# Bank order, copy order and late rounding around the gated block of a fused attention + SwiGLU kernel

## The chip, the cores and the metric

The kernel runs on one core of one Trainium2 chip. The metric is the device time of one launch in microseconds (us), as the median of several runs. The engines are named as in the profile: PE (TensorE: matmuls; PEld is its weight loads), ACT (ScalarE), DVE (VectorE), POOL (GpSimd) and SP (SyncE, which here only issues DMAs).

## The reference

```python
# attention: B, H, S, D = 4, 8, 768, 64; a query sees the keys that fall in its own hash bucket
mask = q_bucket[:, :, :, None] == k_bucket[:, :, None, :]
scores = np.where(mask, scale * (q @ k.T), -1e9)
x = softmax(scores) @ v                 # -> (3072 tokens, 512)
# gated block: w_gate, w_val (512, 1536), w_out (1536, 512), all float64 inputs
g = x @ w_gate
y = (g * (1.0 / (1.0 + np.exp(-g))) * (x @ w_val)) @ w_out     # -> (3072, 512), float32
```

## The kernel before

**Three stages.** Attention comes first (to about 314 us of the profiled span). Then the 3072 tokens go through the gated block in three blocks of 1024: block 0 (314 to 513 us), block 1 (513 to 715 us), and a last block that uses a seven-product scheme with sums of weights and of inputs (715 us to the end). The change touches the gated block alone.

**Split numbers.** A matmul operand is held in three parts along an index v: 0 high, 1 low, 2 their difference ("diff"). A product needs four matmul passes on the parts 0 and 1 ("a") and one set on part 2 ("n"), and the two results are joined as (4096+1)·a − n.

**Order.** The order is written out by hand: every engine runs its instructions in the order in which the Python emits them. A waiting instruction therefore holds back all that is queued behind it on its engine.

**U steps.** A U step (function `up` and the U branch of `atoms_of`) makes 128 columns of gate and value for 1024 tokens. It has four atoms, at = 0 to 3, in the order of PE: a of the gate, a of the value, n of the gate, n of the value. After each a, ACT copies it times −4097 into the bank pair of the same side's n (L847), so that the n matmuls add onto it. After n of the gate, ACT takes its Silu (L860); after n of the value, DVE multiplies it by the gate (L870). Later ACT makes the high part of the hidden value (L879), and DVE the low part and the diff (L890, L893); this "tail" is emitted two atoms after the step.

**D steps.** After every third U step, one U later, a D step multiplies three hidden tiles by three pieces of w_out. It goes through eight chunks c of 128 tokens, nine matmuls each: six into half 0 of a bank pair (a), three into half 1 (n). ACT (L956), or DVE for some parts (L958), evicts half 0 into the running sum, then DVE subtracts half 1 (L962). In block 1, D steps after the first add onto a sum: `sow` has ACT copy −sum into half 1 of the chunk's bank pair before its matmuls (L921), called from `ahead_of["D"]` inside the U step before, from `begin` and from `chunk`. D 3, the last of a block, starts with two of the three j of the first chunks (`begin`), since its third hidden tile is not ready. In what follows, "D 0 of block 1" is the first D step of block 1, and so on.

**Banks.** PSUM is used as four bank pairs, given in turn by `two_banks` (a counter modulo four). A U step takes four, a D step eight, so U always begins at the same pair, called bank 0 here, and chunk c of a D step stands in bank c mod 4. Before, a U step held a of the gate in bank 0, n of the gate in bank 1, a of the value in bank 2, n of the value in bank 3.

**Ring.** Weights come in pieces of 768 KB through a ring of six buffers. `bring` (L308) asks for the next piece on POOL's queue; the request waits until the buffer's last reader is done.

**Sums.** During block 1, DVE also makes the sums of weights (tile `made`, side g and side v, `add`, L1079 to L1088) and of inputs (xa, xb, ya, yb; L1096 to L1102) that the last block needs. ACT rounds their high part (`high`, L1108), DVE the rest (`low`, L1114 or L1116; `diff`, L1123 or L1127), and SP stores them (L1125, 1536 KB; L1129, 768 KB each). There is one `made` buffer for a side, so the next sum of that side waits until the store before has landed. The dictionary `plan`, filled by `put(kind, f, at, op, ...)`, says after which atom each of these is emitted.

**Last block.** `group("g" or "v", p)` runs the seven products A11, S1, S2, A12, S3, S4, A22 with the operands T1 to T4 (loaded by L1177 and L1205) and emits left-over work of the group before at slots 1 to 6 (`then`, `at_slot`).

```python
ahead_of["D"] += [lambda: sow(1), lambda: sow(2 if order[i + 1][1] % 4 < 3 else 3)]   # L1215
tails.append([1 if n % NF == NF - 1 else 2, tail])                                    # L1248
```

Of the kernel before, what the change touches and what calls it, by code (L numbers as in the profile page):

```python
# [19 lines left out]
def kernel(  # L20
# [33 lines left out]
    B, H, S, D = q.shape  # L54
# [12 lines left out]
    NQ = 3  # L67
# [724 lines left out]
    def gated_block(scope):  # L792
# [12 lines left out]
        def mm(ps, w, x, start, stop, **more):  # L805
            nc.tensor.matmul(ps, w, x, start=start, stop=stop, **more)  # L806

        def up(F, what):
            b = F // NF
            w = held[what, F]  # L810
            a, n_ = two_banks("a"), two_banks("n")

            def block(v, j):
                return w[:, v, j * P : (j + 1) * P]

            def first():
                for j in range(NJ):
                    for v in range(2):
                        for half in range(WB // PIECE):
                            mm(a[:, half], block(v, j), r32(xparts[b, j][:, half, v]),  # L820
                               j == 0 and v == 0, j == NJ - 1 and v == 1)

            def second(onto):
                for j in range(NJ):
                    for half in range(WB // PIECE):
                        mm(n_[:, half], block(2, j), r32(xparts[b, j][:, half, 2]),
                           j == 0 and not onto, j == NJ - 1, skip_group_check=onto)

            return first, second, a, n_
# [4 lines left out]
        def atoms_of(kind, n):  # L834
# [66 lines left out]
            else:  # L901
# [24 lines left out]
                def start(c, js, steps=None):  # L926
                    if c not in tiles:
                        tiles[c] = two_banks("o")
                    t = tiles[c]
                    cols = slice(c * P, (c + 1) * P)  # L930
                    def first():
                        for j in js:
                            for v in range(2):
                                mm(t[:, 0], hs[j][:, v, cols], ws[j][:, v],
                                   j == 0 and v == 0, j == nq - 1 and v == 1)

                    def second():
                        for j in js:
                            mm(t[:, 1], hs[j][:, 2, cols], ws[j][:, 2], j == 0 and not onto,
                               j == nq - 1, skip_group_check=onto)  # L940

                    for go in steps or ("ba" if final and c >= ahead else "ab"):
                        (first if go == "a" else second)()

                def end(c):
                    t = tiles.pop(c)
                    early = final and c >= ahead
                    if early:
                        nc.vector.tensor_tensor(accs[c], accs[c], t[:, 1], op=ALU.subtract)
                    if part == 0 or onto:  # L950
                        if part == 0 and c // 2 not in paired:
                            accs[c // 2, "both"] = outp.tile([P, 2, DM], FP32, tag=f"o{c // 2}",
                                                             name="o")
                        if part == 0:
                            accs[c] = accs[c // 2, "both"][:, c % 2]
                        nc.scalar.activation(accs[c], t[:, 0], AF.Copy, scale=STEP + 1)  # L956
                    else:
                        nc.vector.scalar_tensor_tensor(out=accs[c], in0=t[:, 0],  # L958
                                                       scalar=STEP + 1, in1=accs[c],
                                                       op0=ALU.mult, op1=ALU.add)  # L960
                    if not early:
                        nc.vector.tensor_tensor(accs[c], accs[c], t[:, 1], op=ALU.subtract)  # L962
                    if part == NF // nq - 1:
                        batch, at = divmod(b * NCB + c, NCH)
                        if final and c >= ahead:
                            nc.sync.dma_start(rows[batch][:, at, :], accs[c])
                        elif c // 2 in paired:
                            nc.sync.dma_start(rows[batch][:, at - at % 2 : at - at % 2 + 2, :], accs[c // 2, "both"])
                    paired.add(c // 2)
                    if c == NCB - 1:  # L970
                        bring(nq)

                def begin(c):
                    sow(ahead)
                    start(c, range(nq - few))
                    if c == ahead - 1:
                        sow(4)

                for c in range(ahead):
# [27 lines left out]
                for c in turns_:  # L1007
                    if final and c == NCB - 1:
                        yield lambda: last(NCB - 1)
                        return  # L1010
                    if final and c == NCB - 2:
                        last_diffs(NCB - 1)

                    def chunk(c=c):
                        if c >= ahead:
                            start(c, range(nq))
                        else:
                            start(c, range(nq - few, nq), "ab")
                        if ahead and c == 5:
                            sow(7)  # L1020
                        end(c)
                        if not ahead:
                            sow(c + 3)
                        elif c >= ahead:
                            sow(8 if c >= 5 else c + 2)
                    yield chunk

        bring(RINGS[1])
# [116 lines left out]
        for p in range(NG - 1):  # L1145
            g, v = ("w", p, 0), ("w", p, 1)
            F = (LAST - 1) * NF + 2 * p
            put("U", 2 * p, 0, keep_w, "g", F)
            put("U", 2 * p, 1, keep_w, "v", F)
            f = 2 * p + 1  # L1150
            if f % NQ == 0:
                at = [("D", f // NQ - 1, c) for c in range(1, 6)]
            else:
                at = [("U", f + 1, c) for c in range(1, 4)]
                at += [("D", f // NQ, 0), ("D", f // NQ, 1)] if (f + 1) % NQ == 0 else [("U", f + 2, 0), ("U", f + 2, 0)]
            ops = [[(high, g)], [(high, v), (low, g)], [(diff, g)], [(low, v)], [(diff, v)]]
            for here, todo in zip(at, ops):
                for op, key in todo:
                    put(*here, op, key)
# [1 line left out]
        put("U", 4, 2, load_x, LAST, (1, 1 + NP // 2))  # L1161
        xa, xb, ya, yb = (("x", j, side) for j in range(2) for side in range(2))
        for kind, f, at, op, key in (("U", 4, 0, add, xa), ("U", 4, 1, add, xb),
                                     ("U", 4, 2, high, xa), ("U", 4, 3, high, xb),
                                     ("U", 4, 3, low, xa), ("U", 4, 3, diff, xa),
                                     ("U", 5, 0, low, xb), ("U", 5, 0, diff, xb),
                                     ("D", 1, 3, add, ya), ("D", 1, 5, add, yb),
                                     ("D", 1, 5, high, ya), ("D", 1, 7, high, yb),
                                     ("D", 1, 6, low, ya), ("D", 1, 7, diff, ya),
                                     ("U", 7, 0, low, yb), ("U", 7, 0, diff, yb)):  # L1170
            put(kind, f, at, op, key)
# [39 lines left out]
        def sow_next(i):  # L1211
            if i + 1 < len(order) and order[i + 1][0] == "D":
                gens[i + 1] = atoms_of(*order[i + 1])
                sow = next(gens[i + 1])
                ahead_of["D"] += [lambda: sow(1), lambda: sow(2 if order[i + 1][1] % 4 < 3 else 3)]  # L1215

        for i, (kind, n) in enumerate(order):
            b, f = divmod(n, NF if kind == "U" else NF // NQ)
# [19 lines left out]
            for at, atom in enumerate(gens.pop(i, None) or atoms_of(kind, n)):  # L1238
# [12 lines left out]
                if kind == "D" and f == NF // NQ - 1:  # L1251
                    if at == 0:
                        more = [split_x(b + 1, pr) for pr in range(NP // 2, NP)]
                        if b == LAST - 1:
                            for i_ in (1, 2):
                                bring_sum(i_, xparts_p, f"x{i_ - 1}")
                    if b == LAST - 1:
                        if at in (2, 4, 5, 7, 8, 9):
                            more[at in (4, 7, 9)].pop(0)()
                        if at == 7:  # L1260
                            fourth_sum()
                    elif at in (0, 7, 10):
                        for x in more:
                            x.pop(0)()
# [40 lines left out]
        def then(k, op):  # L1305
            after.setdefault(k, []).append(op)
# [5 lines left out]
        def group(what, p):  # L1312
# [125 lines left out]
            then(3, lambda: diff(0))  # L1438
            then(3, lambda: high(1))
            then(4, lambda: low(1))  # L1440
            then(5, lambda: diff(1))

        gates = {}
        assert not tails
# [47 lines left out]
```

## Time and profile before

| what | value |
|---|---|
| median of 3 runs | 905.1 us (904.12 to 906.36) |
| the profiled execution's own time | 903.35 us |
| its span, first to last instruction | 901.3 us |
| PE busy | 891.0 us, 99% |
| DVE busy | 678.9 us, 75% |
| ACT busy | 533.5 us, 59% |
| POOL busy | 106.7 us, 12% |
| granted TensorE clock | 0.999 |
| DMA, all queues | 224.06 MB, mean 249 GB/s |

The span and what lies around it differ by 2.05 us in the profiled execution. A busy engine is one that works on an instruction; a PE matmul of 512 columns counts as about 390 ns although the next one starts 227 ns later (32 matmuls of a U step at 346.68 to 353.93 us), since they overlap in the pipeline. So lost time on PE shows as a start that comes later than 227 ns after the last one, more fully than as idle time.

### The profile page before, as it was taken

Reading aid. Unit: us, or ns where it says so; the run is one execution under the profiler, and the core shown is the slowest. Engines: PE = TensorE matmul, PEld = TensorE weight load, DVE = VectorE, ACT = ScalarE, POOL = GpSimd, SP = SyncE. Lnnn points to the kernel's source line nnn. Section 1 sums busy time; section 2 is a strip of 40 time slices with the busy share of each in tenths; the row PEclk is TensorE's granted clock in tenths of the full one; section 3 lists DMA queues with packets and bytes.
Section 4 is the critical chain, followed back from the end, with each engine's and each line's share of the span. In section 5 each row is a group of like instructions: output and inputs, shape, how many; then the busy total and the mean of one; then the engine's idle time right before and its main releaser. Section 6 shows DMA issues by size and latency. Waiting matters only on the chain.

```text
span 901.3 us, 12795 instructions
## 1 busy us (share of the span) xinstructions
PE 891.0 (99%) x4731; PEld 622.4 (69%) x4731; DVE 678.9 (75%) x877; ACT 533.5 (59%) x782; POOL 106.7 (12%) x211
## 2 busy tenths in 40 slices
PE   9999999999999999999999999999999999999998
PEld 5444444444444487888878788878888777888887
DVE  6779999999988956649473987789793578377486
ACT  7788988788888745442433234446364576376470
POOL 2001100010001210001001000100010122121110
PEclk9999999999999999999999999999999999999999
DMA  7657877887877699685857788797869998297382
GB/s 183 109 148 183 188 205 190 214 217 215 231 193 219 210 361 349 235 301 174 295 194 257 251 342 323 255 348 304 325 266 400 393 357 280 86 350 263 138 300 93
DMA packets 149980, 224.06 MB, mean 249 GB/s; under 512 B 104000, under 2 KB 113696, under 8 KB 148000
## 3 DMA queue, kind: packets, MB, share of 16 engines
q0 software_dynamic: 25312, 128.99, 40.7%
q1 hardware_dynamic: 123200, 93.08, 34.0%
q10 hardware_dynamic: 1408, 1.20, 0.5%
q8 instruction: 37, 0.61, 0.3%
q14 instruction: 23, 0.19, 0.1%
HBM read 157.81 MB, written 64.59 MB: 247 GB/s over the span
## 4 chain that ended last, share of the span: by engine, by line
PE 72%; DVE 12%; issue 8%; DMA 4%; ACT 2%; POOL 1%; SPq 0%; POOLq 0%; DVEq 0%; ACTq 0%
PE sc L605 17%; PE av L636 14%; PE o L806 13%; PE a L806 13%; PE n L806 6%; PE y L806 3%; DMA sums_ram<-made 2%; PE joint L677 1%; DVE hid L1410 1%; PE joint L497 1%; DMA ring<-sums_ram 1%; DVE o L962 1%; DVE made L1114 1%; DVE made L1123 1%; DVE hid L890 1%
## 5 line engine op out<-in xcount | busy, mean ns | idle before, releaser
L806 PE MATMUL o<-ring,hid 128*128 128x512 f32 (+1 forms) x872 | 201.3, 389 | 4.2 <-ACT g L860 2.2
L806 PEld LDWEIGHTS o<-ring,hid 128*128 128x128 f32 x872 | 162.0, 188 | 42.2 <-ACT o L921 3.9
L806 PE MATMUL a<-xparts,ring 128*128 128x512 f32 x768 | 178.1, 389 | 0.0
L806 PEld LDWEIGHTS a<-xparts,ring 128*128 128x128 f32 x768 | 144.1, 188 | 30.5 <-issue 0.6
L615 ACT ACTIVATE A<-sc 128x768 f32<-128x768 f32 x192 | 154.0, 815 | 1.6 <-PE sc L605 0.8
L605 PE MATMUL sc<-qT,kT 64*128 64x384 f32 x768 | 153.0, 483 | 0.0
L636 PE MATMUL av<-A,vraw 128*64 128x386 f32 (+1 forms) x768 | 127.7, 488 | 0.0
L847 ACT ACTIVATE n<-a 128x1024 f32<-128x1024 f32 x46 | 46.3, 1008 | 133.8 <-PE a L806 127.4
L308 POOL DMA_DIRECT2D ring<-ram x108 | 60.3, 560 | 394.5 <-PE o L806 121.6
L636 PEld LDWEIGHTS av<-A,vraw 128*64 128x64 f32 x768 | 53.7, 136 | 73.3 <-issue 62.4
L605 PEld LDWEIGHTS sc<-qT,kT 64*128 64x128 f32 x768 | 68.8, 187 | 39.9 <-issue 35.0
L806 PE MATMUL n<-xparts,ring 128*128 128x512 f32 x384 | 91.5, 390 | 1.2 <-ACT n L847 1.2
L962 DVE TENSOR_TENSOR o<-o 128x512 f32<-128x512 f32 x84 | 57.1, 685 | 36.8 <-PE o L806 18.2
L806 PEld LDWEIGHTS n<-xparts,ring 128*128 128x128 f32 x384 | 71.8, 188 | 17.2 <-ACT n L847 2.4
L956 ACT ACTIVATE o<-o 128x512 f32<-128x512 f32 x56 | 33.4, 597 | 57.1 <-PE o L806 56.9
L890 DVE SCALAR_TENSOR_TENSOR hid<-hid,v 128x1024 fp32r<-128x1024 f32 (+1 forms) x26 | 29.7, 1141 | 47.9 <-ACT hid L879 47.9
L605 PE MATMUL sc<-qb,kb 64*128 64x384 bf16 x384 | 63.5, 323 | 0.0
L659 DVE SCALAR_TENSOR_TENSOR both<-A 128x1536 f32<-128x1536 f32 x32 | 55.4, 1733 | 3.9 <-ACT A L615 2.3
L663 DVE TENSOR_TENSOR both<-both,A 128x1536 f32<-128x1536 f32 x32 | 55.9, 1748 | 1.7
L806 PE MATMUL y<-xparts,ring 128*128 128x512 f32 x216 | 55.0, 390 | 0.0
L806 PEld LDWEIGHTS y<-xparts,ring 128*128 128x128 f32 x216 | 40.5, 188 | 8.8 <-DMA ring<-ram 0.3
L605 PEld LDWEIGHTS <-kb 64*128 64x128 bf16 x384 | 19.6, 94 | 32.5 <-issue 9.0
(219 smaller groups left out, 1074.7 us busy)
## 6 DMA issues: line engine op xcount, KB each, us to landing
ring<-ram POOLq DMA_DIRECT2D x96, 768.0 KB, 6.5
sums_ram<-made SPq DMA_DIRECT2D x12, 1536.0 KB
ring<-sums_ram POOLq DMA_DIRECT2D x24, 768.0 KB, 6.5
ram<-stage POOLq DMA_DIRECT2D x22, 768.0 KB, 4.5
ram<-stage SPq DMA_DIRECT2D x14, 768.0 KB
vraw<-in_v_dram SPq DMA_DIRECT2D x16, 384.0 KB
words<-xram SPq DMA_DIRECT2D x12, 512.0 KB
xsums<-made SPq DMA_DIRECT2D x8, 768.0 KB
```

The source lines that it names most:

```text
L308: nc.gpsimd.dma_start(t.bitcast(FP32)[:, :, cols], src[:, :, cols])
L497: nc.tensor.matmul(tile_[i * BLOCK : (i + 1) * BLOCK, 0:HQ], hash_w, T[name, n][:, half * HQ : (half + 1) * HQ], start=True, stop=True)
L605: nc.tensor.matmul(banks_of[u][:, h], x["k", n][rows, ks], x["q", n][rows, qs], start=start, stop=stop)
L615: nc.scalar.activation(weights(u)[:, :, 0:HQ], banks_of.pop(u), AF.Exp, scale=SCALE * (1.0 if units[u][0] else OFF / 2))
L636: nc.tensor.matmul(ps[h * D : (h + 1) * D, 0:width], raws["v", n][:, h, c, :], a[:, h, 0:width], start=c == 0, stop=c == NCH - 1)
L659: nc.vector.scalar_tensor_tensor(out=t, in0=first, scalar=S * EPS / P / 2, in1=now, op0=ALU.add, op1=ALU.add)
L663: nc.vector.tensor_tensor(t, t, now, op=ALU.add)
L806: nc.tensor.matmul(ps, w, x, start=start, stop=stop, **more)
L847: nc.scalar.activation(n_, a, AF.Copy, scale=-(STEP + 1))
L890: nc.vector.scalar_tensor_tensor(out=l_, in0=h_.bitcast(FP32), scalar=-STEP, in1=v_, op0=ALU.mult, op1=ALU.add)
L956: nc.scalar.activation(accs[c], t[:, 0], AF.Copy, scale=STEP + 1)
L962: nc.vector.tensor_tensor(accs[c], accs[c], t[:, 1], op=ALU.subtract)
```

## The change

It does seven things: (1) a U step holds the two a in banks 0 and 1 and the two n in banks 2 and 3; (2) `sow` emits the copies of the first two chunks ahead of the Silu, the fourth in `begin(0)`, and those of later chunks ahead of the eviction of the chunk in hand; (3) the last chunk of a D step goes j by j through its three w_out pieces, and each piece is given back after its own matmuls; (4) in D 0 and D 2 of block 1 the rounding of the weight sums is emitted one chunk later; (5) the high part of xb moves from step 4 to step 5, its low part and diff from after atom 0 to after atom 1 of step 5; (6) two ACT roundings of inputs in D 3 of block 1 move to earlier atoms; (7) in the last block the second diff moves from slot 5 to slot 6.

```diff
@@ def up(F, what):
-            a, n_ = two_banks("a"), two_banks("n")
+            at = bank[0] + (what == "v")
+            a, n_ = two_banks("a", at), two_banks("n", at + 2)
+            bank[0] += 4 * (what == "v")
@@ def start(c, js, steps=None):
+                    if c == NCB - 1 and not final:
+                        for j in js:
+                            for v in range(2):
+                                mm(t[:, 0], hs[j][:, v, cols], ws[j][:, v],
+                                   j == 0 and v == 0, j == nq - 1 and v == 1)
+                            mm(t[:, 1], hs[j][:, 2, cols], ws[j][:, 2], j == 0 and not onto,
+                               j == nq - 1, skip_group_check=onto)
+                            bring()
+                        return
@@ def end(c):
-                    if c == NCB - 1:
+                    if c == NCB - 1 and final:
                         bring(nq)
@@ def begin(c):
-                    if c == ahead - 1:
+                    if c == 0:
                         sow(4)
@@ def chunk(c=c):
-                        if ahead and c == 5:
-                            sow(7)
+                        if ahead and 3 <= c <= 5:
+                            sow(c + 2)
                         end(c)
                         if not ahead:
                             sow(c + 3)
-                        elif c >= ahead:
-                            sow(8 if c >= 5 else c + 2)
+                        elif c >= 5:
+                            sow(8)
@@ the plan of the sums
             if f % NQ == 0:
-                at = [("D", f // NQ - 1, c) for c in range(1, 6)]
+                at = [("D", f // NQ - 1, c) for c in range(2, 7)]
@@
-                                     ("U", 4, 2, high, xa), ("U", 4, 3, high, xb),
+                                     ("U", 4, 2, high, xa), ("U", 5, 0, high, xb),
                                      ("U", 4, 3, low, xa), ("U", 4, 3, diff, xa),
-                                     ("U", 5, 0, low, xb), ("U", 5, 0, diff, xb),
+                                     ("U", 5, 1, low, xb), ("U", 5, 1, diff, xb),
@@ def sow_next(i):
-                ahead_of["D"] += [lambda: sow(1), lambda: sow(2 if order[i + 1][1] % 4 < 3 else 3)]
+                ahead_of["D"] += [lambda: sow(2), lambda: sow(2 if order[i + 1][1] % 4 < 3 else 3)]
@@ the atoms of D 3 in block 1
-                        if at in (2, 4, 5, 7, 8, 9):
-                            more[at in (4, 7, 9)].pop(0)()
+                        if at in (1, 2, 5, 7, 8, 9):
+                            more[at in (2, 7, 9)].pop(0)()
@@ def group(what, p):
-            then(5, lambda: diff(1))
+            then(6, lambda: diff(1))
```

Number and kind of the instructions are the same before and after; PE's order is the same but for the last chunk of each D step, and what moves is which bank an instruction uses and where ACT, DVE, SP and POOL have their instructions in the queue.

## The prediction

> **What bounds the kernel now.** I began with the page's busy table, which says that PE has hardly any idle time, and went on to the waits of PE.
>
> ```profile
> PE 891.0 (99%) x4731; PEld 622.4 (69%) x4731; DVE 678.9 (75%) x877; ACT 533.5 (59%) x782; POOL 106.7 (12%) x211
> ```
> ```profile
> PE o L806 <- ACT g L860: 2.2, 2, 1.1
> PE o L806 <- ACT o L921: 1.6, 3, 0.8
> PE n L806 <- ACT n L847: 1.2, 2, 1.0
> ...
> PE five__6010 L806 <- DMA ring<-sums_ram: 0.2, 1, 0.2
> ```
> The columns are total, times and longest. The change adds and removes no matmul, so it can only win or lose such waits. I priced them from the starts of matmuls: anything over 227 ns from one start to the next is lost, and after a wait the next matmul is late by a further 0.11 us. From 314 us on they come to about 11.5 us, and that is the most any edit here could win. The places follow from the timeline. First block 0:
>
> ```profile
> 359.25 0.63 ACT L179 ACTIVATE stage<-stage 128x512 fp32r<-128x512 f32 x1 [3.15 <-DVE stage L191]
> 359.79 1.01 ACT L860 ACTIVATE g<-n 128x1024 f32<-128x1024 f32 x1
> 360.85 1.42 PE L806 MATMUL o<-ring,hid 128*128 128x512 f32 x5 [1.09 <-ACT g L860]
> ```
> Columns: start, duration, engine, line, and in brackets the idle time and its releaser. Chunk 1 of D 0 uses the pair that held n of the gate, so PE waits for the Silu, which stands in ACT's queue behind a rounding that waits for DVE. Then U 5 of block 1, on ACT, DVE and again DVE:
>
> ```profile
> 591.36 1.06 ACT L1108 ACTIVATE made<-made 128x1024 fp32r<-128x1024 f32 x1 [5.94 <-DVE made L1102]
> 592.32 1.92 ACT L847 ACTIVATE n<-a 128x1024 f32<-128x1024 f32 x2
> ```
> ```profile
> 588.58 0.69 DVE L1099 TENSOR_TENSOR made<-words 128x512 f32<-128x512 f32 x1 [8.76 <-DMA sums_ram<-made]
> 596.02 1.23 DVE L1127 TENSOR_TENSOR made<-made 128x1024 fp32r<-128x1024 f32 x1
> 597.16 1.22 DVE L890 SCALAR_TENSOR_TENSOR hid<-hid,v 128x1024 fp32r<-128x1024 f32 x1
> 604.43 0.69 DVE L1079 TENSOR_TENSOR made<-ring 128x512 f32<-128x512 f32 x1 [0.84 <-DMA xsums<-made]
> ```
> A store that landed at 588.55 holds DVE, DVE holds the high part of xb, that holds the copy for n of the gate, and PE starts n at 593.4, 1.23 us late. Last, D 3 of block 1:
>
> ```profile
> 704.12 0.60 ACT L956 ACTIVATE o<-o 128x512 f32<-128x512 f32 x1 [1.82 <-PE o L806]
> 704.62 0.60 ACT L921 ACTIVATE o<-o 128x512 f32<-128x512 f32 x1
> 705.27 3.04 PE L806 MATMUL o<-ring,hid 128*128 128x512 f32 x12 [0.84 <-ACT o L921]
> ```
> The copy for chunk 4 stands behind an eviction that itself waits for PE to end chunk 3.
>
> **Part 1, banks.** D 0 and D 2 of block 0 lose 1.25 + 0.11 = 1.36 us each (360.85 and 460.16). Afterwards chunk 1 stands where a of the value stood, which was copied out long before. What is late next is chunk 2 behind the Silu and chunk 3 behind L870: without the wait they start at 361.5 and 363.6, while the Silu ends at 360.80 and L870 at 362.06, so both are hidden by 0.7 and 1.5 us. The start of a U step also finds its pairs in time: n of the gate now needs the pair of chunk 6 where it needed chunk 5's, but not before two a of 32 matmuls, 7.25 us each. Gain 2.72 us.
>
> **Part 5, xb, as far as the end of D 1.** The copy for n of the gate no longer stands behind the high part of xb: 1.23 us won in U 5. But low and diff of xb now come after the tail, L890 and L893 (1.22 + 1.23, so 2.46 us later): the diff ends at about 599.7, not 597.24. Its two stores were issued from 597.30 and landed at 602.00 and 604.31, behind the two of xa (landed 598.19 and 600.09). The first xa store took 3.3 us from issue, and the next landed 1.9 us later; so issued from 599.75, xb's would land at about 604.95. For this landing the next weight sum waits on DVE (604.43 above), and from there DVE works almost without a gap to L962 of D 1's chunk 2 (620.17), behind which come the copy for chunk 6 and PE at 620.86, which already is 0.52 us late there. So the 1.23 us are waited for again in D 1, and its end moves with the landing: by 0.65 us later, say 0.7. The bounds are 0.2 (the xa stores set the pace) and 2.46 (the full delay). I take 0.7 because the two xa stores are the same transfers on a queue as empty.
>
> **Part 4, late rounding, and U 11.** In D 2 of block 1 chunk 4 loses 0.33 us at 666.1, its copy being behind an eviction that is behind a rounding. One chunk later this goes. But the sums' store is then issued about 0.65 us later, as in D 0; the load of words queued behind it on SP (landed 690.02) gates two roundings ahead of U 11's Silu and copy, where PE loses 0.25 us at 692.7. The landing sets the end, so the net is between −0.33 (the load is not later) and +0.65 (all of it); I take +0.3.
>
> **Parts 2, 6 and 3, from D 3 to the last block.** D 3 of block 1 loses 0.25, 1.11 and 0.83 us (701.2, 705.3, 708.9), 2.2 in all. With the copies for chunks 5 to 7 ahead of evictions 3 to 5, and chunk 4's in `begin`, the last two go; about 0.5 stays, as the first wait is behind DVE. Gain 1.7. The added wait is that an eviction now stands behind a copy that waits for DVE's L962 two chunks before; behind the eviction stand the next copy and then PE. In D 3 those L962 are done in time, so I take it as hidden; if DVE were as late as in D 1, 0.4 us of it would come back. The last block then starts at about 713.6, not 715.13 (less the rest), and its first vrow and v12 pieces are needed earlier too. They already cost 0.19 and 0.49 us at 724.7 and 726.6. They are requested at 715.13, 715.88 and 716.46, the last of them 10.1 us before it lands. Given back one by one, the three requests move up, against the matmuls, by 0.9, 0.45 and 0 us. Yet the queues show when they moved: from 713 to 718 only SP's queue did, and then the ring's.
>
> ```profile
> q1 hardware_dynamic: 813, 1.64, 96.6%
> ```
> ```profile
> q0 software_dynamic: 449, 2.30, 81.5%
> q1 hardware_dynamic: 168, 0.58, 20.4%
> ```
> The first fence is 713:718, the second 719:726 (packets, MB, share). While SP's loads and stores fill the engines, an earlier request is worth little. So half of D 3's gain is waited for again at v12: net −0.9, between −2.4 (1.7 kept, and the 0.68 gone) and +1.0 (all eaten, and SP's own loads of operands late).
>
> The Trainium skill, page "DMA: Bandwidth & Descriptors", section "Queues, rings and completion order", says that each DMA engine takes turns between the queues that have work, packet by packet. In the window 582 to 586 both queues indeed moved (1.18 and 0.50 MB), but in 713 to 718 the ring moved nothing though requested. By the rule the earlier pieces would take turns with the operand loads, D 3's gain would be lost to late operands, and the sum would be −1.7.
>
> **Part 7 and the rest of 3.** The five waits of 0.36 us in the last block stand behind low(1) in slot 4, not behind the second diff: nothing. Going j by j adds no wait, as the pair is awaited at the first matmul either way.
>
> **Sum.** −2.72 + 0.7 + 0.3 − 0.9 = −2.6 us: the profiled 903.35 becomes 900.7. The median stands 1.75 above the profiled run, and I take the difference over: 905.1 − 2.6 = 902.5 us.
>
> **Rivals.** *All is kept:* the stores land as before (+0.2), U 11 is not later, and v12's pieces arrive with the earlier start: −2.72 + 0.2 − 1.7 = −4.2, so 900.9. For it speaks that the ring moved at 81.5% of the engines as soon as SP's queue was done; against it, that SP's queue holds the same bytes.
>
> *The store in D 0 of block 1 falls behind ring pieces:* slower. The store of the sums that DVE waits for at 588.58 was issued at 575.76 and took 12.8 us, where the same store issued at 613.78 took 5.3: three ring pieces were requested from 574.13 on. They landed at 581.59, 587.44 and 590.56, the next two at 592.89 and 595.40. With pieces requested earlier (3) and the store later (4), the third and fourth, or the fifth too, go ahead of it: it lands 4.3 to 6.8 us later, and L1099, xb and D 1's end with it. That makes −2.6 + 4.3 to 6.8, or 906.8 to 909.3, say 908.2. It is slower than before from 2.6 us of further delay. Against it: before, the store overtook the third piece, and from 582 to 586 its queue had 69.1% of the engines against the ring's 30.8%.
>
> *Nothing comes of it:* the waits return elsewhere, at DVE or at a load, since PE has no other slack: 905.1 ± 0.5. Part 1 speaks against it, as its two waits have no late producer behind them.
>
> **How the numbers follow.** About 0.3% (2.7 us) is what a measurement of this kernel can tell from no change. The forecast (902.5) has 0.48; it lies on that border, so 0.24 faster, 0.24 same. All is kept: 0.25, with 0.24 faster and 0.01 same. The late store: 0.15, with 0.10 slower and 0.05 same. Nothing: 0.12, all same. Together faster 0.48, same 0.42, slower 0.10. The best ends give −2.72 + 0.2 − 0.33 − 2.4 = −5.25, so 899.8; the worst +1.4, so 906.5. The range from 899.8 to 906.2 leaves out most of the late store and a little on the other side.
>
> **What the profile after would show.** Right: no wait on L860; n of U 5's gate without its wait; D 1 waiting for L921 more than before, by about 1 us; D 3's waits under 0.6; a longer wait at v12. Wrong: a store that lands over 2 us later against PE in D 0 or D 2 of block 1; waits on L860 or L870 at chunks 2 and 3; T4's loads awaited by PE.

## The result, and the profile after

The changed kernel is slower: the median of 15 runs is 906.43 us (905.54 to 909.19), against 903.82 us (901.91 to 906.36) of 15 runs of the kernel before beside them. The ratio is 1.0034 (95% interval 1.0024 to 1.0044), which is 3.1 us of 903.8. The profiled execution took 906.43 us with a span of 904.5 us, where the profile before had 903.35 and 901.3.

PE's share of the page has not moved, and the waits of PE show where the time is (the changed kernel; total, times, longest):

```profile
PE 892.4 (99%) x4731; PEld 624.3 (69%) x4731; DVE 678.8 (75%) x877; ACT 533.7 (59%) x782; POOL 107.0 (12%) x211
```
```profile
PE n L806 <- ACT n L849: 4.4, 2, 4.2
PE o L806 <- DVE hid L892: 1.0, 1, 1.0
...
PE five__6010 L806 <- DMA ring<-sums_ram: 0.7, 1, 0.7
PE o L806 <- ACT o L923: 0.7, 2, 0.4
PE o L806 <- DVE hid L895: 0.3, 1, 0.3
PE o L806 <- DMA ring<-ram: 0.2, 1, 0.2
```

The waits on the Silu are gone and those on copies for chunks (L921, now L923) have shrunk from 1.6 to 0.7. One wait of 4.2 us is new, and stands at a place that the prediction had priced at a fraction of a microsecond. The next table compares the starts of PE's steps in the two traces. PE runs the same steps in the same order, so the shift of the changed kernel against the one before, read at one step and at the next, gives what each stretch won or lost.

| stretch | shift at its end (us) | won or lost | predicted |
|---|---|---|---|
| attention, which the change doesn't touch | +0.35 | +0.35 | 0 |
| block 0 (D 0 and D 2) | −2.44 | −2.79 | −2.72 |
| D 0 of block 1 | −3.02 | −0.58 | 0 |
| U 5 | −4.15 | −1.13 | −1.23 |
| from there to the end of D 1 | −1.06 | +3.09 | +1.93 |
| D 2 | −1.44 | −0.38 | −0.33 |
| U 11 | +4.37 | +5.81 | +0.63 |
| D 3 | +2.30 | −2.07 | −1.7 |
| start of the last block (to v12) | +2.88 | +0.58 | +0.8 |
| rest of the last block | +3.20 | +0.32 | 0 |

Eight of the ten lie within 0.6 us of the forecast. D 1 lost 1.2 us more, and U 11 alone lost 5.8 us, more than all that was won after block 0. The 0.58 us of D 0 don't go with the change: this wait is gone in the trace of d3_only too, whose edit doesn't touch D 0, and stands at 0.50 us in that of load_first, which has the whole change (both kernels below).

**U 11 in the trace.** PE, and then ACT in front of it (timeline of the changed kernel; start, duration, engine, line):

```profile
695.48 5.50 PE L806 MATMUL n<-xparts,ring 128*128 128x512 f32 x16 [4.21 <-ACT n L849]
```
```profile
689.75 0.63 ACT L1199 ACTIVATE xparts<-words 128x512 fp32r<-128x512 f32 x1 [8.32 <-DMA words<-xram]
692.85 0.63 ACT L1199 ACTIVATE xparts<-words 128x512 fp32r<-128x512 f32 x1 [2.46 <-DMA words<-xram]
693.38 1.00 ACT L862 ACTIVATE g<-n 128x1024 f32<-128x1024 f32 x1
694.42 1.01 ACT L849 ACTIVATE n<-a 128x1024 f32<-128x1024 f32 x1
```

ACT stands at two roundings whose words have not landed; behind them, in its queue, are the Silu of U 10 and the copy that U 11's n matmuls add onto. In the kernel before, the same two roundings start 2.8 us earlier, and PE lost 0.25 us there:

```profile
686.94 0.63 ACT L1188 ACTIVATE xparts<-words 128x512 fp32r<-128x512 f32 x1 [4.06 <-DMA words<-xram]
690.04 0.63 ACT L1188 ACTIVATE xparts<-words 128x512 fp32r<-128x512 f32 x1 [2.48 <-DMA words<-xram]
```

PE's line above shows a second loss: 16 matmuls take 5.50 us, where 16 in the same form took 3.92 us in the kernel before (692.68). The windows of the changed kernel tell why (the columns are length, busy time of PE, PEld, DVE, ACT and POOL, the granted clock of PE, the DMA share, GB/s):

```profile
692.36:695.77 3.41, 0.29 (x1) 0.29 (x2) 2.05 (x3) 2.58 (x4) 0.00 (x0) 1.00 1.03 434
695.77:699.18 3.41, 3.41 (x9) 2.64 (x9) 2.41 (x3) 3.06 (x5) 0.00 (x0) 0.50 0.93 377
```

After the wait PE was granted half of its clock for 3.41 us, and seven matmuls came 427 ns apart, not 227, with a partly slow one on either side. So the wait itself cost 4.4 us and the slow clock another 1.7.

**Why the words were late.** The load of words is queued on SP behind the store of sums. The queues from 677 to 680, first of the kernel before, then of the changed kernel (packets, MB, share):

```profile
q1 hardware_dynamic: 64, 0.79, 62.8%
q0 software_dynamic: 66, 0.41, 34.1%
```
```profile
q0 software_dynamic: 166, 0.92, 96.3%
q1 hardware_dynamic: 2, 0.02, 1.9%
```

Before, SP's queue (q1) shared these three microseconds with the ring (q0). In the changed kernel the ring had them alone, although the store was issued at 674.42. POOL's requests and SP's issues show the order that goes with it (timelines of the changed kernel):

```profile
672.07 1.89 POOL L308 DMA_DIRECT2D ring<-ram  x3 [9.38 <-PE o L806]
```
```profile
670.95 3.79 SPq L1136 DMA_DIRECT2D sums_ram<-made  x2
674.79 1.18 SPq L1050 DMA_DIRECT2D words<-xram  x2
```

The second store (674.42) and the loads come after all three pieces (672.07, 672.75, 673.43). The same in the kernel before:

```profile
674.42 1.57 POOL L308 DMA_DIRECT2D ring<-ram  x3 [10.67 <-PE o L806]
```
```profile
671.42 3.79 SPq L1125 DMA_DIRECT2D sums_ram<-made  x2
675.25 0.93 SPq L1039 DMA_DIRECT2D words<-xram  x2
```

There the pieces were requested at 674.42, 674.94 and 675.46 and the second store at 674.88: behind one piece, ahead of two. Two parts of the change had worked on the same gap from both sides: giving pieces back one by one moved the requests 0.6 to 0.9 us up against PE, and the late rounding moved the store 1.0 us back.

### The profile page after: what moved, and what is told of

The parts are those of the page before. It is cut to its first block, busy times and chain, and to the rows that moved or that the text cites. A ratio compares the mean times of both kernels' runs of the same rounds, so it can differ in the third digit from the quotient of the medians.

```text
span 904.5 us, 12799 instructions
## 1 busy us (share of the span) xinstructions
PE 892.4 (99%) x4731; PEld 624.3 (69%) x4731; DVE 678.8 (75%) x877; ACT 533.7 (59%) x782; POOL 107.0 (12%) x211
## 4 chain that ended last, share of the span: by engine, by line
PE 74%; DVE 11%; issue 8%; DMA 5%; ACT 2%; POOL 1%; SPq 0%; POOLq 0%; DVEq 0%; ACTq 0%
PE sc L605 17%; PE av L636 14%; PE a L806 14%; PE o L806 13%; PE n L806 6%; PE y L806 3%; DMA sums_ram<-made 2%; PE joint L677 1%; DMA ring<-sums_ram 1%; DVE o L973 1%; PE joint L497 1%; PE x L806 1%; DVE hid L1421 1%; DVE hid L892 1%; DVE made L1125 1%
## 5 line engine op out<-in xcount | busy, mean ns | idle before, releaser
L892 DVE SCALAR_TENSOR_TENSOR hid<-hid,v 128x1024 fp32r<-128x1024 f32 (+1 forms) x26 | 29.7, 1141 | 47.5 <-ACT hid L881 47.5
L605 PEld LDWEIGHTS <-kb 64*128 64x128 bf16 x384 | 19.6, 94 | 32.5 <-issue 9.0
```

What stands on the lines that cost most here:

```text
L605: nc.tensor.matmul(banks_of[u][:, h], x["k", n][rows, ks], x["q", n][rows, qs], start=start, stop=stop)
L892: nc.vector.scalar_tensor_tensor(out=l_, in0=h_.bitcast(FP32), scalar=-STEP, in1=v_, op0=ALU.mult, op1=ALU.add)
```

## The experiments

Each kernel ran in several rounds beside the kernel before; the ratio is that of the run to it. "Landing" is that of the second load of words. It, the requests of D 2's three ring pieces and the issue of the second store are counted in us from the start of the first matmul of U 10, so that a kernel's earlier gains don't enter.

| kernel | ratio (95% interval) | pieces requested | store issued | landing | PE lost at U 11 |
|---|---|---|---|---|---|
| before | 1 | 0.0, 0.5, 1.1 | 0.47 | 15.6 | 0.3 |
| changed | 1.0034 (1.0024 to 1.0044) | −0.9, −0.2, 0.5 | 1.45 | 19.9 | 6.1 |
| banks_only | 0.9974 (0.9961 to 0.9988) | 0.0, 0.5, 1.1 | 0.49 | 15.6 | 0.3 |
| no_late_round | 1.0016 (1.0003 to 1.0028) | −0.9, −0.2, 0.5 | 0.54 | 18.5 | 3.1 |
| pieces_at_end | 1.0046 (1.0029 to 1.0062) | 0.0, 0.5, 1.1 | 1.44 | 19.5 | 5.7 |
| xb_back | 1.0021 (1.0009 to 1.0033) | −0.9, −0.2, 0.5 | 1.60 | 19.7 | 7.2 |
| neither | 0.9984 (0.9974 to 0.9994) | 0.0, 0.5, 1.1 | 0.55 | 15.8 | 0.5 |
| all_three_back | 0.9961 (0.9945 to 0.9978) | 0.0, 0.5, 1.1 | 0.55 | 15.9 | 0.5 |
| load_first | 0.9965 (0.9952 to 0.9978) | −0.9, −0.2, 0.5 | 1.44 | −9.7 | 0 |
| best | 0.9958 (0.9944 to 0.9972) | 0.0, 0.5, 1.1 | 0.97 | −7.7 | 0 |
| pieces_and_late | 1.0054 (1.0040 to 1.0068) | −0.9, −0.2, 0.5 | 1.44 | 19.6 | 6.8 |
| xb_only | 1.0020 (1.0011 to 1.0029) | 0.0, 0.5, 1.1 | 0.46 | 15.8 | 0.4 |
| xb_high_only | 0.9995 (0.9986 to 1.0003) | 0.0, 0.5, 1.1 | 0.49 | 15.6 | 0.3 |
| d3_only | 0.9990 (0.9980 to 1.0000) | 0.0, 0.5, 1.1 | 0.49 | 15.7 | 0.4 |

**banks_only: the kernel before, with the bank order.**

```diff
-            a, n_ = two_banks("a"), two_banks("n")
+            at = bank[0] + (what == "v")
+            a, n_ = two_banks("a", at), two_banks("n", at + 2)
+            bank[0] += 4 * (what == "v")
```


> The kernel before with the bank order of U steps alone. Theory (each part acts at its own place): the two waits of 1.36 us in D 0 and D 2 of block 0 go and all later work moves up with PE, so 2.7 us faster than before. Rival (the loads keep their own pace): PE comes 2.7 us earlier to the same loads and waits for them at U 11 and at the start of the last block, so under 1 us faster.

Measured: ratio 0.9974, or 2.3 us faster (1.1 to 3.5). Both waits on the Silu are gone from the trace, and U 11 loses no more than before, so the loads moved up with PE. The first theory holds; only at vrow did PE give 0.7 us of it back. (vrow and v12 are the first two products of the last block that read pieces for the value side: six matmuls into the tile y, at 724.73 in the kernel before, and then those into the tile five__6010, at 726.62.)

**no_late_round, pieces_at_end and neither: the changed kernel with one of the two suspects undone, or both.**

```diff
-                at = [("D", f // NQ - 1, c) for c in range(2, 7)]   # no_late_round, neither
+                at = [("D", f // NQ - 1, c) for c in range(1, 6)]
...
-                    if c == NCB - 1 and not final:                  # pieces_at_end, neither:
...                                                                  # the block j by j is left out
-                    if c == NCB - 1 and final:
+                    if c == NCB - 1:
                         bring(nq)
```


> The changed kernel with the roundings of the weight sums in D 0 and D 2 of block 1 back at their old chunks. The changed kernel waits 4.4 us at U 11 and then runs eight matmuls at about half clock. If the late rounding makes the load of words late: the wait goes, 5 to 6 us faster than the changed kernel. If the ring pieces given back one by one make it late: the store is issued 0.7 us earlier but still close behind the third piece, so the wait stays above 3 us and the time within 1 us of the changed kernel.

> The changed kernel with the three ring pieces of a D step requested together after the last chunk. If the pieces make the load of words late: the wait at U 11 goes, 5 to 6 us faster than the changed kernel. If the late rounding does: the wait stays above 3 us and the time within 1 us of the changed kernel. If it takes both, each of these two kernels is 3 to 6 us faster.

> The changed kernel without the pieces given back one by one and without the late rounding. Each alone left the store of D 2's sums behind all three ring pieces. Theory (the place of the store among the requests sets when the words for U 11 land): the store goes back between the first and the second piece, U 11 waits under 0.6 us, no matmul there runs at half clock, and the time is 5 to 6 us below the changed kernel, about 900.5. Rival (the words land late because PE comes earlier to U 11 than the transfers can follow): the wait stays above 2.5 us and the time within 2 us of the changed kernel.

With the old rounding, U 11's loss falls from 6.1 to 3.1 us. The landing is still 2.9 us later than before, and what else went is the slow clock, which did not follow this shorter wait. Its time is 1.6 us less than the changed kernel's, not 5 to 6, as the slow clock came in D 1 instead (below). With the pieces at the end, 5.7 us remain at U 11; the time can't be told from the changed kernel's, though in this trace PE also waits 2.2 us at vrow, with a slow clock behind it. So neither suspect alone is the cause, and the expectation "3 to 6 us each" for the case that it takes both was wrong as well: either one is enough to put the store behind all three pieces. With both undone the landing is back at 15.8, PE loses 0.5 us, and the kernel is 0.5% faster than the changed one (4.5 us, a little less than the 5 to 6 that were expected). ACT's two roundings in the kernel with neither (timeline):

```profile
684.81 0.63 ACT L1190 ACTIVATE xparts<-words 128x512 fp32r<-128x512 f32 x1 [4.25 <-DMA words<-xram]
687.92 0.63 ACT L1190 ACTIVATE xparts<-words 128x512 fp32r<-128x512 f32 x1 [2.48 <-DMA words<-xram]
```

**pieces_and_late: the kernel before with the two suspects alone.** The edit is the reverse of that of the kernel with neither, on the kernel before.

> The kernel before with the two suspects alone: the pieces given back one by one and the late rounding. Theory (they put D 2's store of sums behind all three ring pieces, and the words for U 11 behind the store): U 11 waits 3.5 to 4.5 us, with or without 1.8 us of half clock behind it, so 3 to 6 us slower than before, less what D 0 and D 2 win (0.3). Rival (it takes the earlier start of PE by the bank order too): U 11 waits under 1 us and the time is within 1 us of before.

Measured: 1.0054, 4.9 us slower. U 11 loses 6.8 us without any help from the bank order (waits of PE):

```profile
PE n L806 <- ACT n L847: 5.8, 3, 4.0
PE o L806 <- ACT g L860: 2.2, 2, 1.1
```

The wait of 4.0 us is U 11's, and the two on the Silu are still there. The rival is out. (The first line also holds U 5's wait, 1.7 us in this run.)

**load_first: the changed kernel, with the loads of words ahead of the stores.**

```diff
         put("U", 4, 2, load_x, LAST, (1, 1 + NP // 2))
+        put("D", 2, 0, load_x, LAST, range(NP // 2))
...
                 if kind == "U" and f == NF - 2:
                     assert not made
-                    load_x(LAST, range(NP // 2))
```


> The changed kernel, whole, with one thing moved: the two loads of words for U 11 are emitted after the first atom of D 2, so that on SP's queue they stand ahead of the two stores of sums. Theory (U 11 waits only because these loads stand behind the late store): the wait of 4.4 us and the half clock go, 5 to 6 us below the changed kernel, about 900.5. Rival (the transfers as a whole are late, whatever their order): PE waits for ring pieces in U 10, U 11 or D 3 instead, and no more than 3 us are won.

Measured: 0.9965, median 900.34 us, some 6 us below the changed kernel. SP's issues in this kernel (timeline):

```profile
653.34 2.42 SPq L1050 DMA_DIRECT2D words<-xram  x2
670.63 0.32 SPq L1136 DMA_DIRECT2D sums_ram<-made  x1
```

The loads are now issued some 21 us earlier. The stores are as late as in the changed kernel (the second lands 13.3 against 13.5 us after U 10's start), and from 676 to 679 the ring again moved alone (1.03 MB, SP's queue 0.00), but nothing that PE needs stands behind the store: U 11 loses nothing. The same bytes move, so the loss was the load's place in SP's queue, and not the amount of transfers.

**xb_back, all_three_back, xb_only and xb_high_only: the place of xb's rounding.** xb_back and all_three_back undo the new place in the changed kernel and in the kernel with neither; xb_only puts it into the kernel before; xb_high_only moves the high part and leaves low and diff.

```diff
-                                     ("U", 4, 2, high, xa), ("U", 4, 3, high, xb),
+                                     ("U", 4, 2, high, xa), ("U", 5, 0, high, xb),   # both
...
-                                     ("U", 5, 0, low, xb), ("U", 5, 0, diff, xb),
+                                     ("U", 5, 1, low, xb), ("U", 5, 1, diff, xb),    # xb_only
```


> The changed kernel with the rounding of xb back at its old places. Theory (D 1's end follows the landing of xb's stores): U 5 waits 1.2 us again, but D 1 ends some 2 us earlier against block 0, so about 2 us faster than the changed kernel. Rival (D 1's new waits come from the order of the copies or of the pieces): U 5's wait comes back and D 1's stay, so about 1.2 us slower.

> As the kernel with neither, and with the rounding of xb at its old places too. Theory: U 5 waits 1.2 us, D 1 ends 2 us earlier against block 0, so 1 to 2 us below the kernel with neither, about 899. Rival (what D 1 wins is waited for at U 11 or in the last block, at loads that keep their pace): within 0.5 us of the kernel with neither.

> The kernel before with the rounding of xb moved as in the changed kernel, alone. Theory (D 1's end follows the landing of xb's second pair of stores, which stands 2.5 us of DVE work later): U 5's wait goes, D 1's waits grow by 2.5 to 3.2 us, so 1.3 to 2 us slower than before at D 1's end. Rival (the predicted 0.65 us): 0.7 us slower.

> The kernel before with the high part of xb alone moved behind U 5's copy; its low part and diff stay ahead of the tail. Theory (the landing of xb's stores sets D 1's end, and it does not move): U 5's 1.2 us are won and waited for again in D 1, within 0.4 us of before. Rival (a won wait is won): 1.2 us faster.

What each did to D 1 is read as above, as the growth of the shift against the kernel before, from the start of U 4 (574 us) to the end of D 1 (625 us), so that U 5's win is counted against D 1's loss. The last column is the landing of xb's last store, counted from the same start and also against the kernel before (30.18 us there):

| kernel | xb's low and diff | to the end of U 5 | to the end of D 1 | xb's last landing |
|---|---|---|---|---|
| changed | after the tail | −1.17 | +1.96 | +1.96 |
| load_first | after the tail | −1.24 | +1.36 | +1.36 |
| neither | after the tail | −1.28 | +0.93 | +0.94 |
| xb_only | after the tail | −1.28 | +1.15 | +1.16 |
| xb_back | before it | +0.05 | +0.09 | +0.10 |
| all_three_back | before it | +0.03 | +0.03 | +0.01 |
| xb_high_only | before it | −1.28 | −0.11 | −0.11 |
| best (below) | before it | −1.28 | +0.05 | +0.05 |
| d3_only (below) | before it | −1.28 | −1.33 | −1.30 |

The end of D 1 follows this landing to 0.04 us, in the four traces that are not in the table as well, but for no_late_round: its landing came 1.80 us later, and D 1's end 2.73, as the slow clock is in it.

With low and diff after the tail D 1 ends 0.9 to 2.0 us later (2.1 in pieces_at_end); with them before it, it ends where the landing stands. Where the landing came later by itself, in banks_only and pieces_and_late, the end moved by 0.6 and 0.8 us too. In time, xb_only is 0.20% slower (1.8 us, 1.0 to 2.6); at D 1's end its trace gives 1.15 us, between the rival's 0.7 and the theory's 1.3 to 2. all_three_back is 0.23% below the kernel with neither, more than the 0.9 us between their traces at D 1, though the intervals overlap a little.

xb_back was only 1.2 us below the changed kernel rather than 2. In its trace the 1.9 us won by D 1's end are lost again: 1.2 in D 2, where DVE's next weight sum waited 0.98 us for a store of sums that landed 7.7 us after its issue (5.6 before; why is not known), and 1.2 at U 11, most of it by a slow clock that lasted longer (13 matmuls 427 ns apart, where the changed kernel had 7).

xb_high_only cannot be told from the kernel before (1 lies inside its interval): U 5's wait went, and at the end of D 1 nothing of it was left. So a wait won in U 5 is worth nothing as long as the landing of xb's stores sets D 1's end and stays where it is. How, DVE's timeline of the changed kernel shows:

```profile
595.83 1.23 DVE L1138 TENSOR_TENSOR made<-made 128x1024 fp32r<-128x1024 f32 x1
...
603.37 0.69 DVE L1090 TENSOR_TENSOR made<-ring 128x512 f32<-128x512 f32 x1 [2.42 <-DMA xsums<-made]
...
606.17 1.22 DVE L892 SCALAR_TENSOR_TENSOR hid<-hid,v 128x1024 fp32r<-128x1024 f32 x1
607.42 1.22 DVE L895 TENSOR_TENSOR hid<-hid 128x1024 fp32r<-128x1024 f32 x1
```
```profile
607.44 0.96 PE L806 MATMUL o<-ring,hid 128*128 128x512 f32 x3 [1.02 <-DVE hid L892]
608.70 10.72 PE L806 MATMUL o<-ring,hid 128*128 128x512 f32 x46 [0.30 <-DVE hid L895]
```

The diff of xb ends at 597.06, its last store lands at 603.25, the next weight sum (L1090) waits for that, and behind the sum in DVE's queue stands the tail of U 5, L892 and L895, which D 1 needs as its third hidden tile. That is where PE stood.

**d3_only: the kernel before with the new order in D 3 of block 1.**

```diff
-                    if c == ahead - 1:
+                    if c == 0:
                         sow(4)
...
-                        if ahead and c == 5:
-                            sow(7)
+                        if ahead and 3 <= c <= 5:
+                            sow(c + 2)
...
-                        elif c >= ahead:
-                            sow(8 if c >= 5 else c + 2)
+                        elif c >= 5:
+                            sow(8)
...
-                        if at in (2, 4, 5, 7, 8, 9):
-                            more[at in (4, 7, 9)].pop(0)()
+                        if at in (1, 2, 5, 7, 8, 9):
+                            more[at in (2, 7, 9)].pop(0)()
```


> The kernel before with the copies ahead of evictions and the two moved roundings in D 3 of block 1, alone. Theory: D 3's waits fall from 2.2 to about 0.5 us and half of the 1.7 us is waited for again at the vrow and v12 pieces, so 0.9 us faster. Rivals: all of it is kept, 1.7 us faster; or all of it is waited for again at those pieces, whose landing goes by the queue and not by the request, and the time is that of before.

Measured: 0.9990 (0.9980 to 1.0000), so 0.9 us faster, though the interval reaches no change. The waits of PE in this kernel:

```profile
PE y L806 <- DMA ring<-ram: 0.9, 1, 0.9
PE five__6010 L806 <- DMA ring<-sums_ram: 0.6, 1, 0.6
PE o L806 <- ACT o L921: 0.2, 1, 0.2
```

L921 has fallen from 1.6 to 0.2, and vrow and v12 cost 2.0 us with what follows a wait (0.7 before): 1.7 us were won in D 3 and 1.3 of them waited for again, which leaves 0.45.

The trace can't divide the 0.9 further: it is of one of the fastest of the twelve runs (901.45 us, median 902.67) and lacks U 5's wait, which the edit doesn't touch and which came out between 0 and 1.9 us (1.2 before, 1.8 in banks_only, 1.9 in pieces_and_late). What went with it is the order of requests at D 0 of block 1. In this trace the store of sums was issued 0.94 us after U 4's start, ahead of the third ring piece (1.05), and landed at 11.93; in all thirteen other traces it was issued behind all three pieces (1.64 us in the kernel before) and landed at 14.3 to 15.1. So the step between two landings shows a second time, at another store, without an edit to it.

**best: what the runs before it favoured, together.** Bank order, copies and D 3 of the changed kernel; pieces and late rounding as before; the loads of words ahead as in load_first; xb as in xb_high_only.

> Bank order, copies for chunks and the D 3 order from the changed kernel; pieces and late rounding as before; the loads of words for U 11 ahead of D 2's stores; the high part of xb behind U 5's copy as in the changed kernel, but its low part and diff ahead of the tail as before. Theory (each term at its place): 2.7 from block 0, 1.2 from U 5 with D 1 ending as early as the kernel before or earlier, 0.3 at U 11 and 1.7 in D 3, less up to 1 at the start of the last block: 5 to 6 us below the kernel before, about 898. Rival: U 5's gain is waited for in D 1 at DVE, whatever the order, so 4 us below, about 899.5.

Measured: 0.9958, median 900.36 us, 3.8 us below the kernel before, and no better than load_first or all_three_back. It was to reach 898; the 3.8 us are what the rival said, and as it said U 5's win is waited for in D 1 (+0.05 at its end). In this trace D 2 also lost 1.1 us, where the kernel before lost 0.36, behind a store of sums that landed as late as in xb_back. The last block starts at 710.46 (715.13 before), and then PE waits at vrow:

```profile
722.09 1.65 PE L806 MATMUL y<-xparts,ring 128*128 128x512 f32 x6 [1.41 <-DMA ring<-ram]
723.80 1.19 PE L806 MATMUL five__6010<-xparts,ring 128*128 128x512 f32 x4
```

In load_first, neither, all_three_back, best and d3_only the last block starts between 710.5 and 711.7, and v12's first matmul (five__6010) starts between 722.9 and 724.4. From D 3's end to there, 11.5 us in the kernel before become 12.4 to 13.3. What is won ahead of this point is now in part waited for at ring pieces. That their landing is the next bound fits all five; nothing was tried to move them.

## Why the prediction was wrong, step by step

The forecast was 2.6 us faster, in a range to 906.2; measured by the ratio it is 3.1 us slower, and the median of 906.43 lies outside the range. The 905.1 us that the forecast started from, a median of three runs, was also 1.3 us above the 903.82 of the fifteen, but that hid a part of the miss and didn't make it. One step failed, and one more term, that of xb, was too small by 1.3 us.

- **Banks: right.** 2.72 us forecast, 2.79 in the trace, 2.3 as a ratio alone. The "7.25 us each" is a slip that cost nothing: the 32 matmuls from 346.68 to 353.93 us are both a's of a U step, since a takes two passes (parts 0 and 1) and n one, not four and one set as the section on the kernel has it.
- **The step that failed: part 4 at U 11.** It said that the store "is then issued about 0.65 us later" and the load "queued behind it" lands as much later, "so the net is between −0.33 and +0.65". The chain (store, load, two roundings, Silu, copy, PE) was named rightly. But the bound took the delay of an issue for the delay of a landing, and left out part 3: the earlier requests of the pieces were priced at the last block alone, while at U 11 they cost 2.9 us even with the store issued as before (no_late_round, 0.54 against 0.47). The net was +5.4 us, −0.38 in D 2 and +5.81 at U 11. Between two queues the landing goes by what has been requested ahead: over the kernels with loads behind the store it stands at 15.6 to 15.9 us while the store comes behind one or two pieces, and at 18.5 to 19.9 behind all three. The step between these, not the 0.65 of the issue (which came out as 0.98), was the price: 4.2 us, and 1.7 more by the slow clock, which no term held. The prediction's own sign of being wrong, a store that lands over 2 us later against PE in D 2, is what the trace shows: 13.5 us after U 10's start, 9.3 before.
- **The rival that was right in kind and wrong in place.** The late store behind ring pieces was priced at 4.3 to 6.8 us of delay, and put at D 0 of block 1, with 0.15. But there the store already stood behind all three pieces before (575.76, after 574.13, 574.65 and 575.17), the fourth and fifth were still requested over 7 us after it in the changed kernel, and against PE it landed only 0.4 us later. That it landed ahead of the third piece before doesn't say that it had overtaken anything: ahead of that piece's request, in d3_only, it lands 2.5 us earlier. In D 2 it stood 0.06 us ahead of the second piece and 0.58 ahead of the third. The rows for this were in the trace of before; the prediction applied them to the place with the long transfer, not to the place with the small margin.
- **xb: mechanism right, term mis-sized.** 0.7 us forecast for D 1's end (0.2 to 2.46); 0.9 to 2.1 measured where no slow clock came into it, 1.96 in the changed kernel. Of the 1.3 us above the forecast in the changed kernel, 0.4 are the pair's issue, late because D 0's store and xa came 0.4 later, and 0.9 its landing: the two xa stores that were taken for it need 5.2 us from the first issue to the last landing, xb's needed 6.1 (597.12 to 603.25), with a ring piece requested at 598.76 beside them. That PE would wait at L921 was only part of it; most was the tail of U 5 behind the sum on DVE.
- **D 3 to the last block: near.** −0.9 forecast; −1.5 in the trace of the changed kernel, −0.45 in that of d3_only. Copies ahead of evictions cost nothing in D 3.
- **The second diff and j by j: right** that neither adds a wait of its own in its place; the price of the pieces came at SP's queue, where part 3 had not looked.
- **The rule on turns between queues** of the Trainium skill (page "DMA: Bandwidth & Descriptors", section "Queues, rings and completion order") was to show at T4's loads. No wait for them appears. But it doesn't describe 677 to 680 of the changed kernel, where the ring alone moved for three microseconds with a store already issued; from 680 to 690 both queues did move (54.7% and 46.6%).

## What to carry to other kernels

Where one engine's loads stand behind its stores, the place of the store among the requests of other queues sets when the loads land (here 15.6 to 15.9 us, or 18.5 to 19.9); ask of every edit that moves a request or a store whether it changes that order, and price the landing from a row that has the new order. A wait won ahead of a step that a landing or a full queue sets is worth nothing until the landing moves too. Issue the load that PE will need before the store that nobody needs soon: one moved line turned the changed kernel from 0.34% slower into 0.35% faster than the kernel before.

## What was not expected of the hardware

After a wait of over 4 us PE ran at about half its clock: in four kernels, after waits of 4.0 to 4.4 us at U 11, 7 to 13 matmuls came 427 ns apart, and in pieces_at_end 7 more did so after 2.2 us at vrow. The 3.0 us of no_late_round at U 11 drew none. The Trainium skill (page "TensorE: Matmul & The Clock Gate", section "Part 1: The HAM clock gate") says that the clock falls to half after an idle window of about 3.4 us; the waits of 4 us agree. But in D 1 of no_late_round the longest wait was 1.24 us, within four that come to 2.6 us in under 5, and the clock fell all the same. The traces show what decides. Within a trace the stretches at half clock begin and end on a grid of steps of 3.41 us (the two of pieces_at_end begin at 695.78 and 729.92, ten steps apart). These are four steps of no_late_round's grid (columns as above), two in D 1 and two at U 11:

```profile
604.91:608.33 3.42, 1.89 (x7) 0.80 (x6) 3.39 (x5) 1.46 (x2) 0.53 (x1) 1.00 0.89 266
608.33:611.74 3.41, 3.41 (x9) 2.64 (x10) 3.41 (x4) 1.09 (x2) 0.53 (x1) 0.50 0.81 275
690.25:693.66 3.41, 1.76 (x8) 1.13 (x6) 0.90 (x2) 1.46 (x2) 0.00 (x0) 1.00 1.03 433
693.66:697.07 3.41, 2.23 (x10) 1.85 (x11) 2.36 (x2) 3.07 (x5) 0.00 (x0) 1.00 0.99 410
```

The busy time of PE is modelled, and 1.89 and 1.76 us don't tell the first of each pair apart. Counted by late starts, PE lost 2.25 us of the step at 604.91, and the next was slow. At U 11 the longer wait lies across two steps, 1.81 and 1.29 us, and neither was followed by a slow one. In all fourteen traces, from the gated block on, every step at full clock that lost 2.25 us or more was followed by one at half clock (six steps), and none that lost 1.82 or less was. The 1.82 is the changed kernel's D 1, with nearly the same four waits as no_late_round: there the grid cuts them otherwise. So in these traces it is the share of one step that counts, and where a wait falls on the grid, not the length of a wait. An idle window of the full 3.4 us, as the page has it, was not needed. No run was made to test this.
